# One load moved to another queue, and two groups of VectorE instructions put in another order, in a kernel of linear attention and an MLP

## The chip, the cores and the metric

The kernel runs on one core of a Trainium2 chip. The metric is the device time of one execution in microseconds (us). TensorE (PE in the profile) multiplies matrices, VectorE (DVE), ScalarE (ACT) and GpSimd (POOL) do elementwise work, and SyncE (SP) issues most of the transfers. Each engine runs its own list of instructions in order; engines meet only at semaphores.

## The reference

Inputs are q, k, v of shape (4, 8, 768, 64) in float32 (batch, heads, sequence, head size), one decay `lam` per head, and two weight matrices of 512 x 2048 and 2048 x 512. Attention is linear with decay, in blocks of 64 positions; its output, 3072 tokens of 512 features, goes through an MLP with SiLU:

```python
for b in range(nb):
    intra = np.einsum('bhic,bhjc->bhij', qb, kb) * Dmask[None]
    intra = np.einsum('bhij,bhjd->bhid', intra, vb)
    inter = np.einsum('bhid,bhde->bhie', qb * lam_pow[None], kv_state)
    out[:, :, sl] = intra + inter
    kv_state = lam_block[None, :, None, None] * kv_state + np.einsum('bhsd,bhse->bhde', kb_dec, vb)
...
h = x @ w_in
return (h * (1.0 / (1.0 + np.exp(-h)))) @ w_out
```

## The kernel before

**Tiles.** The 3072 tokens are 24 chunks of 128 (6 per batch entry), and 12 groups of 256 tokens (two chunks) for the MLP. Group g holds chunks 2g and 2g+1. Everything is written out by hand in one order per engine (`tc.manual_schedule()`, line 70): the Python code calls the instructions in the order in which each engine will run them, and nothing is rearranged afterwards.

**Chunks 0 to 3** and groups 0 and 1 go by a list (`ORDER`, line 23). From chunk 4 on the attention of a chunk has these steps:

- *Loads.* `load_qk` (line 884) and `load_v` bring q, k and v of a chunk, 256 KB each, into the buffers `qf`, `kf`, `vf`. By default SyncE issues them; with `e=nc.scalar` ScalarE does, from its own instruction list (line 232). The semaphores of the transfers are used in turn, so that an issue may wait until an earlier transfer with the same semaphore has landed.
- *Preparation.* `prep` (line 377) lets GpSimd scale q and k by powers of the decay into `qb` and `kb`: two instructions each (lines 364 and 365).
- *Transposes.* `dma_t` (line 386) lets SyncE transpose `qb` and `kb` by transfer into `qt` and `kn` (lines 390 and 391). They and the loads stand in one list on SyncE.
- *Values.* `vcast` (line 382) casts v to `vb`, on ScalarE, or on GpSimd for chunks 10 and 11.

**`section`** (line 438) emits the attention's matmuls, all at line 540. For `scores` it computes `sp` from `kn` and `qt` and then multiplies by the mask on VectorE into `ss` (line 560). For `states` it computes key-value products `kv_ps` and lets `sums` (line 565) add them on VectorE to the running state `total` (lines 572 and 574), which is cast to `kvs`. For `outs` it multiplies `ss` by `vb` and `qt` by `kvs` into `op`; that is then copied to `xt`, the input of the MLP. With `defer=True` the sums aren't emitted at once; the caller gets the function and calls it later, and the casts `late` are done later still.

**The MLP of a group** has eight steps `ups` (line 955), each with 16 matmuls (two halves of 8) into a bank `h_ps` (line 613; two banks, tag `h`), and Silu on ScalarE into `g` (line 625). As `g` tiles come, VectorE makes sums and differences of them: `g_diff` (line 715, tile `gd`, line 720) and `g_cross` (line 702, tiles `gc`, line 706, and `gb`, line 708). Steps i = 0, 1, ... 7 take the tiles in the order 0, 1, 4, 5, 2, 3, 6, 7; `g_cross` follows steps 3 and 7, `g_diff` steps 1, 3 and 5. Then `seven` (line 735) does the second product by seven products of half the size, with precomputed sums of weights (`wsum`): products 3 and 4 from `g`, 1 from `gc`, 6 and 7 from `gd`, 5 and 2 from `gb`, all at line 733, 8 matmuls each. VectorE and ScalarE combine them: after product 4, ScalarE copies product 3 to `msum` (line 762), VectorE adds product 4 (line 767) and does the last `g_diff`; after product 6 it adds product 1 (line 771). Product 5 accumulates into the bank of product 3, next to product 4.

**The order around the change.** While groups 0 and 1 finish their second product, chunks 4 to 9 are loaded: chunks 8 and 9 by ScalarE's queue (lines 938 and 947). At line 944 chunks 6 and 7 are prepared and transposed. The loop at line 965 then runs group g's MLP with the attention of the next group between its steps. For g = 2, chunks 8 and 9 are prepared and transposed ahead of step 4 (lines 969, 970), and the section for the scores and states of chunks 6 and 7 stands between products 4 and 1 (line 996), its casts on ScalarE. For g = 3, the section for the scores and states of chunks 8 and 9 stands between steps 5 and 6, with the sums deferred to behind step 6 (lines 977 to 980); their casts on ScalarE come between products 4 and 1. In every group the section that makes the next group's `xt` (and, from g = 3 on, the scores and states of the two chunks after it) stands ahead of product 2 (line 1003).

Of the kernel before, what the change touches and what calls it, by code (L numbers as in the profile page):

```python
# [36 lines left out]
def kernel(  # L37
# [10 lines left out]
    nc = tc.nc  # L48
    B, H, S, D = q.shape
# [126 lines left out]
    def move(e, dst, src):  # L176
        if e == "A":
            nc.scalar.activation(dst, src, AF.Copy)  # L178
        elif e == "P":
            nc.gpsimd.tensor_copy(dst, src)  # L180
        else:
            nc.vector.tensor_copy(dst, src)  # L182
# [44 lines left out]
    rawq, rawk, vraw = {}, {}, {}  # L227

    def load_1(src, c, tag, bufs, e=None):
        b, blk = divmod(c, NB)  # L230
        t = io.tile([128, H, D], F32, name=tag, tag=tag, bufs=bufs)
        (e or nc.sync).dma_start(out=t, in_=src[b, :, blk * BLK:(blk + 1) * BLK, :].rearrange("h s d -> s h d"))
        return t

    def load_k(c, e=None):
        rawk[c] = load_1(k, c, "kf", 6, e)
# [198 lines left out]
    LAG = 220  # L435
    T64 = 32

    def section(outs=(), scores=(), states=(), e="AA", tags=(("att", 3),) * 2, spare=None, cast="D", defer=False):

# [20 lines left out]
        states = [(c, h) for c, h in states if (c + 1) % NB or not h]  # L462
# [9 lines left out]
        def place(c, h):  # L472
            w = [x for x, y in states if y == h].index(c)
            return kv[0][:, h] if shared else kv[h][:, w]
# [72 lines left out]
        if outs:  # L547
            if len(outs) == 2:
                x = xt[group_of[outs[0]][0]]
            for i, op in enumerate(banks):  # L550
                if len(tags) == 4:
                    i, w = divmod(i, 2)
                    move(e[w], x[:, 2 * i:2 * i + 2, BLK * w:BLK * w + BLK], op[:, :, 0, :])
                else:
                    move(e[i], x[:, 2 * i:2 * i + 2, :], op.rearrange("d p w s -> d p (w s)"))
        if scores:
            both = []
            for j, sp in enumerate(sps):
                ss = work.tile([128, len(scores) * NP, D], BF16, name="ss", tag="ss", padded_shape=[128, 2 * NP, D])
                nc.vector.tensor_tensor(ss, sp.rearrange("k w p q -> k (w p) q"),  # L560
                                        mask64[:, None, :].to_broadcast([128, len(scores) * NP, D]), op=AL.mult)
                both.append(ss)
            for w, c in enumerate(scores):
                st[c] = [ss[:, NP * w:NP * w + NP, :] for ss in both]
        def sums():
            casts = []
            for c, h in states:
                b = c // NB
                kvs = nat.tile([128, NP, D], BF16, name="kvs", tag="kvs", bufs=8)
                old, total[b] = total.get(b), nat.tile([128, NP, D], F32, name="total", tag="total", bufs=4)  # L570
                if old is None:
                    nc.vector.tensor_copy(total[b], place(c, h))
                else:
                    nc.vector.tensor_tensor(total[b], old, place(c, h), op=AL.add)  # L574
                casts.append((kvs, total[b]))
                if not defer:
                    move(cast, *casts[-1])
                kvh[(c, 1) if h == 0 else (c + 1, 0)] = kvs
            return casts

        if defer:
            return sums
        sums()

    kvh = {}
    mask64 = const.tile([128, 64], F32, name="mask64")
# [128 lines left out]
    def g_diff(g, j):  # L715

        one = quad(g, j)
        d = sum_tile(g, "gd", j // 2, 128)[:, j % 2]
        a, b = (hi, lo) if j < 2 else (lo, hi)
        nc.vector.tensor_tensor(d, one[:, :, a], one[:, :, b], op=AL.subtract)  # L720
        for u in range(4):
            gs[g, 6 if j < 2 else 7, 4 * (j % 2) + u] = d[:, u, :]
# [12 lines left out]
    def seven(g):  # L735

        last = g == len(GROUPS) - 1
        if last:
            tags = ("o0", 1), ("o1", 1), ("att", 3), ("att", 3), ("h", 2)
# [24 lines left out]
        def after_4():  # L764
            if not last:
                after_3()
            nc.vector.tensor_tensor(m, m, place[4], op=AL.add)
            g_diff(g, 3)

        def after_1():  # L770
            nc.vector.tensor_tensor(m, m, place[1], op=AL.add)
# [31 lines left out]
        if last:  # L803
            order = [(3, True, after_3), (4, True, after_4), (1, True, after_1), (6, True, None),
                     (2, False, last_2), (5, False, last_5), (7, True, last_7)]
        else:
            order = [(3, True, None), (4, False, after_4), (1, True, None), (6, False, after_1),
                     (5, False, None), (2, False, after_2), (7, True, after_7)]

        def step(n, start, after):  # L810
# [73 lines left out]
    def load_qk(*cs, e=None):  # L884
        for c in cs:
            if c < NCHUNK:
                rawq[c] = load_1(q, c, "qf", 4, e)
                load_k(c, e)
                loaded.append(c)
# [31 lines left out]
    def down0(kk, *mts):  # L921
        for mt in mts:
            ffn2(mt // 2, mt % 2, range(4 * kk, 4 * kk + 4), tag="h" if mt > 1 else "o")
# [19 lines left out]
    down0(3, 3)  # L943
    preps(6, 7), transposes(6, 7)
    section((4, 5), (), (), "AD", (("att", 3), ("kv", 1), ("att", 3), ("att", 3)))
    down0(3, 0)
    load_qk(9, e=nc.scalar)
    down0(3, 1)
    for i in range(len(WSUMS)):
        weight_sum(i, 1)  # L950
# [1 line left out]
    def steps(*cs):  # L952
        return [(c, h) for c, h in [(cs[0] - 1, 1)] + [(c, h) for c in cs for h in range(2)] if c > 5][:-1]
# [11 lines left out]
    for g in range(2, len(GROUPS) - 1):  # L965
        c, d, a, b = range(2 * g + 2, 2 * g + 6)
        for i in range(8):
            if g == 2 and i == 4:
                preps(8, 9)
                transposes(8, 9)  # L970
                load_qk(10)
                load_vs(8, 9)
                load_qk(11)
            if g < 4 and i in (4, 5):
                vcast(c + i % 2)
            if g == 3 and i == 6:
                sums = section((), (c, d), steps(c, d), defer=True)
            ups(g, i)
            if g == 3 and i == 6:
                late = sums()  # L980
        for i, unit in enumerate(seven(g)):
            if i == 2 and g > 3:
                vcast(a)
            if i == 2 and g == 3:
                for x in late:
                    move("A", *x)
            if i == 2:
                if g == 3:
                    vcast(a, "P"), vcast(b, "P")
                preps(c + 4, d + 4)  # L990
                transposes(c + 4, d + 4)
                load_qk(*([12] if g == 2 else []), c + 7)
                load_vs(c + 6, d + 6)
                load_qk(d + 7)
            if i == 2 and g == 2:
                section((), (c, d), steps(c, d), cast="A")
            if i == 3 and g > 3:
                vcast(b)
            if i == 0 and g == 2:
                load_vs(10, 11)  # L1000
            if i == 5:
                cs = [x for x in (a, b) if g > 2 and x < NCHUNK]
                section((c, d), cs, steps(*cs) if cs else (), "AD", many[:2] if cs else many, cast="P")
            unit()
    g = len(GROUPS) - 1
# [34 lines left out]
```

## Time and profile before

| | us |
|---|---|
| median of 3 runs | 200.37 |
| lowest and highest | 199.79, 200.69 |
| the profiled execution | 199.81 |
| its span | 198.0 |
| TensorE busy in the span | 188.6 |
| VectorE busy | 133.7 |
| ScalarE busy | 100.9 |
| GpSimd busy | 73.3 |

The profile is of one execution. A row of the timeline has the start, the length, the engine (PEld loads weights; ACTq and SPq are the queues from which ScalarE and SyncE issue transfers), the line and the operation with its output and input, and in brackets the idle time ahead of it with what ended that. Rows of equal instructions that follow each other are merged, with x and their count. Lengths in the timeline include the overlap with the next instruction. The chain of work that ended last has the start, the length and the instruction that the end depended on at that time; there the lengths add up. The waits view has, for a waiting instruction and the one it waited for, the total in us, how often, and the longest. In the DMA view the last number is the time from issue to landing. The granted clock of TensorE was full throughout.

### The profile page before, as it was taken

The numbers are of one execution on the slowest core, as the hardware profiler recorded it, in microseconds if no ns is written. First come the engines' busy times: TensorE is split into PE (matmuls) and PEld (weight loads), VectorE is DVE, ScalarE is ACT, GpSimd is POOL, SyncE is SP. The second block draws the span as 40 slices with busy tenths as digits, with TensorE's granted clock in tenths as the row PEclk, the third lists the DMA queues.
The fourth block names the chain that finished last, engine by engine and source line by source line (L and its number), as shares of the span: only waits on it lengthen the run. The fifth ranks groups of instructions, "written<-read, shape, count | busy, mean of one in ns | idle before, by whom it ended". The sixth has DMA issues, their size and how long they took to land.

```text
span 198.0 us, 6672 instructions
## 1 busy us (share of the span) xinstructions
PE 188.6 (95%) x2844; PEld 151.2 (76%) x2844; DVE 133.7 (68%) x254; ACT 100.9 (51%) x190; POOL 73.3 (37%) x126
## 2 busy tenths in 40 slices
PE   7589999999899998999999999999999999999993
PEld 2368544556787887888888888888888888888882
DVE  0796358679996495984765874895885846745443
ACT  2875875162835653554554563563662662633621
POOL 5240000937942463873614751770850300200000
PEclk9999999999999999999999999999999999999999
DMA  3999999999958998999869999599799850200203
GB/s 92 336 353 403 398 408 333 220 288 281 191 83 198 205 138 198 221 128 211 179 121 244 119 225 173 114 267 162 179 377 243 208 196 7 106 0 3 106 3 106
DMA packets 95581, 38.71 MB, mean 196 GB/s; under 512 B 80960, under 2 KB 88640, under 8 KB 95552
## 3 DMA queue, kind: packets, MB, share of 16 engines
q1 hardware_dynamic: 91248, 37.24, 77.0%
q10 hardware_dynamic: 4304, 1.05, 2.9%
q8 instruction: 22, 0.36, 0.7%
q14 instruction: 7, 0.06, 0.1%
HBM read 27.27 MB, written 6.29 MB: 169 GB/s over the span
## 4 chain that ended last, share of the span: by engine, by line
PE 79%; DVE 11%; SPq 3%; DMA 2%; issue 1%; POOL 1%; ACT 1%; DVEq 0%; POOLq 0%
PE h_ps L613 32%; PE o_ps L733 25%; PE o_ps L658 7%; PE h_ps L847 5%; PE op L540 4%; SPq L224 3%; DVE wsum L689 2%; DMA pair<-in_q_dram 2%; PE o_last L733 2%; DVE gd L720 2%; DVE gb L708 1%; PE sp L540 1%; DVE total L574 1%; DVE ss L560 1%; DVE gc L706 1%
## 5 line engine op out<-in xcount | busy, mean ns | idle before, releaser
L613 PE MATMUL h_ps<-xt,w_in_bf 128*128 128x256 bf16 x672 | 76.1, 272 | 0.8 <-ACT g L625 0.8
L613 PEld LDWEIGHTS <-w_in_bf 128*128 128x128 bf16 x672 | 65.5, 98 | 9.6 <-issue 1.0
L625 ACT ACTIVATE g<-h_ps 128x512 bf16<-128x512 f32 x84 | 49.8, 597 | 34.7 <-PE h_ps L613 34.6
L180 POOL CAST kvs<-total 128x256 bf16<-128x256 f32 x26 | 10.7, 416 | 36.9 <-DVE total L574 27.5
L720 DVE TENSOR_TENSOR gd<-g 128x512 bf16<-128x512 bf16 x40 | 21.7, 557 | 3.4 <-ACT g L625 3.4
L364 POOL TENSOR_TENSOR qb<-qf,lam_fwd 128x256 bf16<-128x256 f32 x18 | 12.8, 709 | 28.5 <-DMA qf<-in_q_dram 21.7
L178 ACT ACTIVATE xt<-op 128x256 bf16<-128x256 f32 (+1 forms) x18 | 8.3, 486 | 22.9 <-PE op L540 22.5
L182 DVE CAST xt<-op 128x256 bf16<-128x256 f32 (+1 forms) x16 | 8.3, 543 | 16.4 <-PE op L540 14.8
L706 DVE TENSOR_TENSOR gc<-g 128x512 bf16<-128x512 bf16 x20 | 10.0, 498 | 13.7 <-ACT g L625 13.6
L733 PE MATMUL o_ps<-w_out_bf,gb 128*128 128x256 bf16 x144 | 18.9, 273 | 0.1
L733 PE MATMUL o_ps<-wsum,gd 128*128 128x256 bf16 x144 | 18.7, 273 | 0.0
L733 PE MATMUL o_ps<-wsum,g 128*128 128x256 bf16 x144 | 17.2, 273 | 0.0
L708 DVE TENSOR_TENSOR gb<-g 128x1024 bf16<-128x1024 bf16 x20 | 17.2, 859 | 0.0
L733 PEld LDWEIGHTS <-gd 128*128 128x128 bf16 x160 | 15.7, 98 | 1.8
L733 PEld LDWEIGHTS <-g 128*128 128x128 bf16 x160 | 15.7, 98 | 1.8
L733 PEld LDWEIGHTS <-gb 128*128 128x128 bf16 x160 | 14.8, 98 | 2.3 <-issue 0.3
L364 POOL TENSOR_TENSOR kb<-kf,lam_bwd 128x256 bf16<-128x256 f32 x20 | 15.0, 748 | 2.2 <-DMA kf<-in_k_dram 1.1
L574 DVE TENSOR_TENSOR total<-total,kv_ps 128x256 f32<-128x256 f32 x33 | 13.8, 419 | 2.2
L658 PE MATMUL o_ps<-w_out_bf,g 128*128 128x512 bf16 x64 | 14.8, 379 | 0.0
L365 POOL TENSOR_TENSOR kb<-kf,lam_bwd 128x256 bf16<-128x256 f32 x20 | 14.8, 740 | 0.0
L365 POOL TENSOR_TENSOR qb<-qf,lam_fwd 128x256 bf16<-128x256 f32 x18 | 13.0, 724 | 0.0
L560 DVE TENSOR_TENSOR ss<-sp,mask 128x512 bf16<-128x512 f32 x20 | 12.8, 681 | 0.2 <-PE sp L540 0.2
(106 smaller groups left out, 245.8 us busy)
## 6 DMA issues: line engine op xcount, KB each, us to landing
vf<-in_v_dram SPq DMA_DIRECT2D x20, 256.0 KB, 4.6
kf<-in_k_dram SPq DMA_DIRECT2D x18, 256.0 KB, 5.2
pair<-in_moe_w_out_dram SPq DMA_DIRECT2D x8, 512.0 KB, 7.7
qf<-in_q_dram SPq DMA_DIRECT2D x16, 256.0 KB, 4.3
pair<-in_moe_w_in_dram SPq DMA_DIRECT2D x6, 512.0 KB, 7.1
out_dram<-pair SPq DMA_DIRECT2D x12, 256.0 KB, 3.4
out_dram<-ob SPq DMA_DIRECT2D x10, 256.0 KB, 2.9
pair<-in_k_dram SPq DMA_DIRECT2D x4, 256.0 KB, 4.5
```

The source lines that it names most:

```text
L180: nc.gpsimd.tensor_copy(dst, src)
L364: eng.tensor_tensor(dst[:, 0::2], src[:, 0::2, ::-1, :], by[:, 0::2, ::-1, :], op=AL.mult)
L365: eng.tensor_tensor(dst[:, 1::2], src[:, 1::2], by[:, 1::2], op=AL.mult)
L560: nc.vector.tensor_tensor(ss, sp.rearrange("k w p q -> k (w p) q"), mask64[:, None, :].to_broadcast([128, len(scores) * NP, D]), op=AL.mult)
L574: nc.vector.tensor_tensor(total[b], old, place(c, h), op=AL.add)
L613: nc.tensor.matmul(hps[g, i][:, a:a + 256], lhsT=w_in_bf[:, ko, m * 128:(m + 1) * 128], rhs=xt[g][:, ko, :], start=(ko == 0 and u == 0), s ...
L625: nc.scalar.activation(gg.rearrange("p u n -> p (u n)"), hps[g, i], AF.Silu)
L658: nc.tensor.matmul(o, lhsT=gt[g, ko][:, mt * BLK:(mt + 1) * BLK], rhs=w_out_bf[:, ko, :], start=(ko == 0), stop=(ko == KO_OUT - 1))
L706: nc.vector.tensor_tensor(cross, low[:, :, lo], one[:, :, hi], op=AL.add)
L708: nc.vector.tensor_tensor(both, low, one, op=AL.add)
L720: nc.vector.tensor_tensor(d, one[:, :, a], one[:, :, b], op=AL.subtract)
L733: nc.tensor.matmul(dst, lhsT=lhsT, rhs=rhs, start=(start and k == 0), stop=(k == K2 - 1), skip_group_check=True)
```

## The change

Three edits, none of which adds or removes arithmetic.

1. The k load of chunk 9 is issued by SyncE and not by ScalarE. Its place in SyncE's list is behind the transposes of chunks 6 and 7 and ahead of those of chunks 8 and 9. The q load of chunk 9 stays with ScalarE, in the same place of its list.
2. In the section for chunks 6 and 7 (g = 2) VectorE does the three state sums ahead of the two masks, and the last `g_diff` of the group, which stood ahead of both, now follows both.
3. In g = 3 the deferred state sums of chunks 8 and 9 (four) are emitted behind step 7 and not behind step 6, so that `gc` and `gb` of step 7 come ahead of them on VectorE.

The instruction lists of TensorE and GpSimd have the same instructions in the same order as before; ScalarE's has one transfer less, SyncE's one more.

```diff
-    def section(outs=(), scores=(), states=(), e="AA", tags=(("att", 3),) * 2, spare=None, cast="D", defer=False):
+    def section(outs=(), scores=(), states=(), e="AA", tags=(("att", 3),) * 2, spare=None, cast="D", defer=False, early=False):
...
-        if scores:
+        def masked():
             both = []
...
+        if early:
+            sums()
+        if scores:
+            masked()
         if defer:
             return sums
-        sums()
+        if not early:
+            sums()
...
             nc.vector.tensor_tensor(m, m, place[4], op=AL.add)
-            g_diff(g, 3)
+            if g != 2:
+                g_diff(g, 3)
...
-            order = [(3, True, None), (4, False, after_4), (1, True, None), (6, False, after_1),
+            order = [(3, True, None), (4, False, after_4), (1, True, (lambda: g_diff(g, 3)) if g == 2 else None), (6, False, after_1),
                      (5, False, None), (2, False, after_2), (7, True, after_7)]
...
     section((4, 5), (), (), "AD", (("att", 3), ("kv", 1), ("att", 3), ("att", 3)))
+    rawq[9] = load_1(q, 9, "qf", 4, nc.scalar)
     down0(3, 0)
-    load_qk(9, e=nc.scalar)
+    load_k(9)
     down0(3, 1)
...
             ups(g, i)
-            if g == 3 and i == 6:
+            if g == 3 and i == 7:
                 late = sums()
...
             if i == 2 and g == 2:
-                section((), (c, d), steps(c, d), cast="A")
+                section((), (c, d), steps(c, d), cast="A", early=True)
```

## The prediction, made blind

> **What bounds the kernel now.** I read the page first: its span and the chain that ended last. The profiled execution took 199.81 us, of which the span is 198.0 and 1.8 lies around it.
>
> ```profile
> span 198.0 us, 6672 instructions
> ...
> PE 79%; DVE 11%; SPq 3%; DMA 2%; issue 1%; POOL 1%; ACT 1%; DVEq 0%; POOLq 0%
> ```
>
> TensorE holds 79% of the chain, VectorE 11%. An edit that touches no matmul can only win time where TensorE waits, or where VectorE is the chain. So the second view is TensorE's waits; asked for 41 to 77 us, it has these three rows.
>
> ```profile
> PE h_ps L613 <- ACT g L625: 0.8, 1, 0.8
> PE o_ps L733 <- DVE gc L706: 0.6, 1, 0.6
> PE op L540 <- ACT kvs L178: 0.2, 1, 0.2
> ```
>
> Each of the three edits aims at one of these rows; I price them in order of time from the timeline and the chain. I call the three places A (49 us), B (61 us) and C (74 us). From 77 us to the end the same view, asked for that window, names no TensorE wait, so what is won at A to C stays, if the loads keep up.
>
> **The change part by part.**
>
> *Place A: k of chunk 9 leaves ScalarE's queue.* Timeline, and the landing of one load from the DMA view:
>
> ```profile
> 42.76 0.54 ACTq L232 DMA_DIRECT2D kf<-in_k_dram  x1
> ...
> 47.41 1.91 PE L613 MATMUL h_ps<-xt,w_in_bf 128*128 128x256 bf16 x16
> ...
> 49.05 0.37 ACTq L232 DMA_DIRECT2D kf<-in_k_dram  x1
> 49.47 1.08 ACT L625 ACTIVATE g<-h_ps 128x512 bf16<-128x512 f32 x2 [3.14 <-PE h_ps L613]
> ...
> 50.12 5.64 PE L613 MATMUL h_ps<-xt,w_in_bf 128*128 128x256 bf16 x48 [0.79 <-ACT g L625]
> ```
>
> ```profile
> kf<-in_k_dram ACTq DMA_DIRECT2D x1, 256.0 KB, 6.2
> ```
>
> The k load of chunk 9 shares a semaphore with the k load of chunk 8, and waits for it: that one was issued at 42.76 and took 6.2, so it landed at 48.96; the next issue follows at 49.05. Silu stands behind it in ScalarE's order and starts at 49.47. TensorE's first h tile (8 of the 16 matmuls of the 47.41 row, half of 1.91) was ready about 48.4, so the profile's releaser for the 3.14 is misleading. Without the load, Silu runs from about 48.4 and lasts half of 1.08; its bank is free at 49.0, before TensorE's second tile ends at 49.3. The 0.79 us goes, at no cost on ScalarE. It costs SyncE one issue, priced below. What is late next is VectorE, which runs without a pause from 48 to 61 us; hence place B.
>
> *Place B: state sums of 6 and 7 ahead of the masks, g_diff behind both.* The chain, with the unstalled section of chunks 4, 5 first, then timeline rows:
>
> ```profile
> 44.94 0.80 PE op L540 x64
> ...
> 55.60 1.51 DVE gd L720 x2
> ...
> 57.45 0.60 DVE gb L708
> 58.05 0.33 DVE msum L767
> 58.38 0.34 DVE gd L720
> 58.72 1.20 DVE ss L560 x2
> 59.92 0.34 DVE total L572
> ...
> 61.19 0.42 ACT kvs L178
> ```
>
> ```profile
> 57.54 0.38 ACT L762 ACTIVATE msum<-o_ps 128x256 f32<-128x256 f32 x1 [1.15 <-PE o_ps L733]
> ...
> 60.78 0.25 PE L540 MATMUL op<-ss,vb 64*64 64x64 bf16 x8
> ...
> 62.20 1.05 PE L733 MATMUL o_ps<-w_out_bf,gb 128*128 128x256 bf16 x8
> ```
>
> The section's 64 matmuls take 0.80 when nothing is late; here 1.42 pass between 60.78 and 62.20, so 0.62 is stall, for the last of three casts kvs behind the three totals. With A gone TensorE is at the section at 60.78 - 0.79 = 59.99. VectorE's new order is msum, three totals (59.92 to 61.17: 1.25), masks (1.20), gd (0.34).
>
> If VectorE came no earlier than before, msum would end at 58.38, the totals at 59.63, the masks at 60.83: TensorE waits there, the section ends 0.8 later at 61.63 and not 62.20, and A and B together win 0.57. That is the low bound. But kb of chunk 9 must now wait for a later load (below), so GpSimd pauses from 55 to about 57 us. The two gd at 55.60 cost 0.76 each beside GpSimd's work and 0.34 alone at 58.38: 0.84 less; a little of the gb ahead too, about 0.2. VectorE is then through gb at about 57.0. ScalarE's msum copy (57.54 - 0.79 + 0.33 = 57.08) comes just behind, so msum ends at 57.4, the totals at 58.7, the masks at 59.9, and the last kvs at 59.1. All precede 59.99. I take the full 0.62; it has 0.1 us to spare. The moved gd is ready at 60.3 and is read at about 61.7 (a product of 8 matmuls behind the one at 62.20 - 1.41), so the move itself is free; were it late, it would cost what it is late.
>
> *Place C: gc and gb ahead of the state sums of 8 and 9.*
>
> ```profile
> 68.99 1.02 DVE gb L708
> ...
> 72.72 0.34 DVE total L574
> ...
> 74.41 0.35 DVE gc L706
> ```
>
> ```profile
> 71.19 1.36 POOL L180 CAST vb<-vf 128x512 bf16<-128x512 f32 x2
> ...
> 72.04 0.60 ACT L625 ACTIVATE g<-h_ps 128x512 bf16<-128x512 f32 x1 [0.22 <-PE h_ps L613]
> ...
> 74.80 0.61 PE L733 MATMUL o_ps<-wsum,gc 128*128 128x256 bf16 x4 [0.62 <-DVE gc L706]
> ...
> 76.12 1.04 PE L733 MATMUL o_ps<-w_out_bf,gb 128*128 128x256 bf16 x8
> ```
>
> Four totals (72.72 to 74.41: 1.69) stand ahead of gc, and TensorE waits 0.62 for it. In the new order that wait goes: gc can start when Silu of the last tile ends (72.04 + 0.55). But the first matmul with gb, at 76.12, waits for VectorE's msum (it accumulates into a bank that msum reads; the built program has this wait), and msum still stands behind the totals. VectorE now idles until that Silu instead of doing totals. On the new clock (1.41 earlier): Silu ends at 71.2; gc 0.35, gb 0.60, totals 1.69, msum 0.33 end at 74.2 when GpSimd is quiet. GpSimd isn't: its two casts of vb (71.19 to 72.55) don't move earlier, and lie on gc and gb; gd and gb cost 0.42 more each when beside GpSimd (0.76 against 0.34, 1.02 against 0.60), so the other end is 75.0. TensorE wants 76.12 - 0.62 - 1.41 = 74.09. The new wait is 0.1 to 0.9; I take 0.5, the middle. C wins 0.62 - 0.5 = 0.1, with bounds 0.5 and -0.3.
>
> *The Trainium skill on this place:* SBUF — State Buffer, section Who interferes with whom, says that a VectorE instruction with two SBUF inputs contends with a GpSimd instruction that reads SBUF, and that the later one is fully blocked until the other ends. The 0.76 against 0.34 agrees that there is contention; no row says how much a cast blocks. By that rule gc and gb could each lose a whole cast; that is the second rival.
>
> *What the moved load does to SyncE.* SyncE issues in order and without a pause here; timeline, then landings:
>
> ```profile
> 52.30 1.22 SPq L391 DMA_TRANSPOSE kn<-kb  x1
> ...
> 58.41 1.20 SPq L391 DMA_TRANSPOSE kn<-kb  x1
> 59.65 0.58 SPq L232 DMA_DIRECT2D qf<-in_q_dram  x1
> ...
> 72.94 1.21 SPq L391 DMA_TRANSPOSE kn<-kb  x1
> ```
>
> ```profile
> 56.03 0.79 POOL L365 TENSOR_TENSOR kb<-kf,lam_bwd 128x256 bf16<-128x256 f32 x1
> ...
> 77.49 0.22 PE L540 MATMUL sp<-qt,kn 64*64 64x64 bf16 x2
> ```
>
> ```profile
> qf<-in_q_dram SPq DMA_DIRECT2D x1, 256.0 KB, 3.2
> kn<-kb SPq DMA_TRANSPOSE x1, 2.4
> ```
>
> The load goes out at 53.6, behind the transposes of 6 and 7. The nearest row is the q load at 59.65, also right behind four transposes: 3.2 to land, so 56.8. The far row is the 6.2 above: 59.8. GpSimd then makes kb of 9 in about 1.2 (the 56.03 row ended at 56.82 before, and would end at 58.0), SyncE transposes it (the 58.41 row), and all later loads and transposes queue behind. Their delay d is 0.6 (one issue of 0.58) if SyncE is the limit, a little below zero if the wait inside the earlier transposes absorbs it; it grows to landing minus 57.2 when the load is late (59.8 gives 2.6). The first consumer that can feel d is the scores of chunks 10, 11: the last transpose for them was issued at 72.94 and landed at 75.34; TensorE's matmuls on it begin about 77.49. So there are 2.1 us of slack, which the win uses up: **no more than 2.1 - d can be won**, 1.5 with d = 0.6.
>
> **Sum:** 0.79 + 0.62 + 0.1 = 1.5, and the load's limit is 1.5 as well. Against the profiled 199.81 that is 198.3. The median of the runs shown, 200.37, lies 0.56 above that execution, so the median should fall to 198.9.
>
> **Rivals.**
>
> 1. *The late load becomes the bound, slower than before.* Place: GpSimd's kb of 9, then SyncE's transpose of it, then the scores of 10, 11. It decides the sign where d passes 2.1, that is where the load lands after 59.3, 5.7 us behind its issue. With the 6.2 of the row above d is 2.6 and the time 0.5 longer: 200.3, or 200.9 as a median. For it: that very row. Against: it was taken among the loads of chunks 6 to 8, the 3.2 in the emptier stretch where the load now goes. 7%. A milder case, landing at 58 to 59, leaves 0.3 to 1.3: about 199.0, median 199.6. 13%.
> 2. *A new wait at C eats A's win.* If gc and gb each wait for a whole cast (1.36 for the two, in place of the 0.4 of my middle case), msum ends about 75.6, TensorE waits 1.5, C loses 0.9, and 0.5 is left: 199.3, median 199.8. For it: the casts stay where they are while VectorE comes earlier. Against: only one cast may overlap. 12%.
> 3. *The change doesn't do what it says*: VectorE, not the load or the order, still ends the stretch to 61 us, because GpSimd's pause doesn't help it. A and B give 0.57, C 0.1: 199.1, median 199.7. 10%.
> 4. *All three waits vanish* (0.79 + 0.62 + 0.62 = 2.0; d near zero, casts off gc and gb): 197.8, median 198.4. 10%.
>
> **How the numbers follow.** My forecast, a win of 1.1 to 1.9, holds 48%. A measurement of this kernel can tell 0.5%, about 1.0 us, from no change. Faster by more: the forecast, rival 4 and half of the milder case of rival 1, 65%. Within: rivals 2 and 3 and the other half, 28%. Slower: 7%. The predicted time is 198.9. The range goes from 198.0 (rival 4, with the scatter of the runs, which reach 0.6 below their median) to 200.2 (the mild cases of rivals 1 to 3); outside it stay the slower case and a few in a hundred on either side.
>
> **What would show it.** Right: no ScalarE DMA issue at 49 us and Silu near 48.4; no TensorE wait at 50.1; the section of 6 and 7 in 0.8 to 0.9; the wait for gc gone, and a TensorE wait of up to 0.9 for msum ahead of the first matmul with gb of the next group; kb of 9 on GpSimd near 57. Wrong: kb of 9 later than 58.5, or TensorE waiting for a transpose at the scores of 10, 11 or 12, 13: then the load costs more than I took. A wait ahead of the section of 6 and 7 for the masks would say that VectorE did not gain from GpSimd's pause. If the waits went as forecast and the time did not, a load further on must have come late.

## The result, and the profile after

| | before | after |
|---|---|---|
| median, us (13 runs each) | 199.54 | 198.70 |
| lowest | 198.76 | 197.94 |
| profiled execution | 199.81 | 198.77 |
| its span | 198.0 | 196.9 |

The ratio is 0.9941 with an interval of 0.9916 to 0.9966: faster by 1.2 us (0.7 to 1.7). Ratios here leave out, on both sides, the executions more than 1.5% above the fastest of their kernel, so they need not be the quotient of two medians: these two medians differ by 0.8, and in the repeat below (a2_again), where four of 12 are out against two of 35, the medians hardly differ. The prediction was 198.9, with a range of 198.0 to 200.2. The 0.59% lies just over the 0.5% that a measurement can tell from no change; the interval reaches below that mark.

In the changed kernel the lines have other numbers: h_ps 619 (before 613), Silu 631 (625), the second product 739 (733), `gc` 712 (706), `gb` 714 (708), `gd` 726 (720), `msum` 773 (767), the totals 573 and 575 (572 and 574). One figure of the section on the kernel needs mending: a step of the MLP has 8 matmuls in two halves of 4, not 16 (a group's eight steps are the x64 below); the prediction's working uses 8.

The page of the changed kernel, its chain by engine:

```profile
span 196.9 us, 6669 instructions
...
PE 85%; DVE 5%; SPq 2%; DMA 2%; issue 2%; POOL 1%; ACT 1%; DVEq 0%; POOLq 0%
```

VectorE's share of the chain fell from 11% to 5%, TensorE's rose from 79% to 85%. TensorE's waits of the changed kernel from 44 to 82 us (waiting instruction, what it waited for, us in total, times, longest):

```profile
PE o_ps L739 <- DVE msum L773: 0.3, 1, 0.3
PE o_ps L664 <- issue: 0.2, 1, 0.2
```

The three waits of before are gone (for `g`, `gc` and `kvs`), and the new one for `msum` that the prediction named is there. Next, the timeline of the changed kernel through places A and B:

```profile
47.97 7.39 PE L619 MATMUL h_ps<-xt,w_in_bf 128*128 128x256 bf16 x64
49.05 0.60 ACT L631 ACTIVATE g<-h_ps 128x512 bf16<-128x512 f32 x1 [2.16 <-PE h_ps L619]
...
52.73 0.53 SPq L232 DMA_DIRECT2D kf<-in_k_dram  x1
...
54.30 0.41 DVE L712 TENSOR_TENSOR gc<-g 128x512 bf16<-128x512 bf16 x1
54.63 0.68 DVE L714 TENSOR_TENSOR gb<-g 128x1024 bf16<-128x1024 bf16 x1
55.24 0.75 DVE L726 TENSOR_TENSOR gd<-g 128x512 bf16<-128x512 bf16 x2
55.75 0.71 POOL L364 TENSOR_TENSOR kb<-kf,lam_bwd 128x256 bf16<-128x256 f32 x1 [1.65 <-DMA kf<-in_k_dram]
56.02 0.72 DVE L712 TENSOR_TENSOR gc<-g 128x512 bf16<-128x512 bf16 x1
56.42 0.79 POOL L365 TENSOR_TENSOR kb<-kf,lam_bwd 128x256 bf16<-128x256 f32 x1
56.66 1.10 DVE L714 TENSOR_TENSOR gb<-g 128x1024 bf16<-128x1024 bf16 x1
...
59.26 1.28 DVE L560 TENSOR_TENSOR ss<-sp,mask 128x512 bf16<-128x512 f32 x2
...
60.59 0.25 PE L540 MATMUL op<-ss,vb 64*64 64x64 bf16 x8
61.37 1.05 PE L739 MATMUL o_ps<-w_out_bf,gb 128*128 128x256 bf16 x8
```

Place A is one row: 64 matmuls without a gap (how much of this is owed to the change is told with b2 and b3). Silu follows the first tile at 49.05, 1.08 behind its start. Between GpSimd's instructions VectorE runs fast (54.30 to 55.99); from 55.75 on k of chunk 9 is on GpSimd, and `gc` and `gb` of the last step take 0.72 and 1.10 instead of 0.41 and 0.68. That makes the masks end at 60.54, and the section's matmuls on `ss` start at 60.59. Place C of the same timeline:

```profile
71.83 0.42 DVE L712 TENSOR_TENSOR gc<-g 128x512 bf16<-128x512 bf16 x1 [0.49 <-ACT g L631]
72.17 0.68 DVE L714 TENSOR_TENSOR gb<-g 128x1024 bf16<-128x1024 bf16 x1
72.56 0.76 POOL L180 CAST vb<-vf 128x512 bf16<-128x512 f32 x1 [0.82 <-DMA vf<-in_v_dram]
72.77 1.78 DVE L575 TENSOR_TENSOR total<-total,kv_ps 128x256 f32<-128x256 f32 x4
73.33 1.21 SPq L391 DMA_TRANSPOSE kn<-kb  x1
74.46 0.41 DVE L773 TENSOR_TENSOR msum<-msum,o_ps 128x256 f32<-128x256 f32 x1
74.93 1.03 PE L739 MATMUL o_ps<-w_out_bf,gb 128*128 128x256 bf16 x8 [0.28 <-DVE msum L773]
```

VectorE idles until Silu, does `gc` and `gb` undisturbed, then the four totals and `msum`; TensorE waits 0.28 for that.

**A table by stage.** For all traces I cut the time by the starts of TensorE's rows. *Start* is the first h matmul of group 2 (47.41 before, 47.97 after). A runs from there to product 3 of group 2 (55.60 and 55.20); B from its product 5 to its product 2 (59.82 to 62.20, 59.42 to 61.37); C from product 1 of group 3 to its product 5 (73.58 to 76.12, 72.74 to 74.93); D from there to its product 2; *rest* from there to the end of the span. The stretches between A and B (4.22) and between B and C (11.37 or 11.38) are the same (within 0.01) in all traces but three: e10_split and e8_early (5.05 and 5.83 between A and B) and e6_late (13.19 between B and C). The runs are those of the experiments.

| trace | start | A | B | C | D | rest |
|---|---|---|---|---|---|---|
| before | 47.41 | 8.19 | 2.38 | 2.54 | 2.20 | 119.68 |
| after | 47.97 | 7.23 | 1.95 | 2.19 | 2.19 | 119.78 |
| a2_again | 49.60 | 7.23 | 1.83 | 2.19 | 2.19 | 119.96 |
| b2 | 48.98 | 7.22 | 2.96 | 2.26 | 2.20 | 119.68 |
| b3 | 47.72 | 9.38 | 2.39 | 2.49 | 2.19 | 119.83 |
| b_delay | 48.75 | 7.96 | 2.39 | 1.83 | 2.19 | 119.38 |
| e1_load | 47.43 | 7.22 | 2.54 | 2.14 | 2.20 | 120.48 |
| e2_section | 47.52 | 8.13 | 2.29 | 2.60 | 2.19 | 120.07 |
| e3_sums | 48.99 | 7.23 | 2.39 | 2.19 | 2.19 | 119.51 |
| e12_no_sums | 49.90 | 7.22 | 1.84 | 2.27 | 2.19 | 119.48 |
| e9_msum | 47.96 | 7.22 | 1.84 | 1.74 | 2.80 | 119.94 |
| e8_early | 47.42 | 7.23 | 1.74 | 2.40 | 2.83 | 121.38 |
| e6_late | 47.45 | 7.23 | 1.98 | 2.60 | 2.19 | 119.64 |
| e10_split | 47.80 | 7.23 | 1.74 | 1.74 | 2.97 | 119.99 |

In the pair before and after, A won 0.96, B 0.43 and C 0.35: 1.74 between 47 and 78 us. Of that, 0.56 was lost ahead of 47 us, where no instruction was changed, and 0.10 behind 78 us; 1.1 is left, as the spans say. These are differences of two single executions; means over the traces stand further down, under the sum. The start is scatter of single executions: group 0's h matmuls begin between 17.21 and 18.78 in the traces of before and of kernels with its code ahead of them, between 17.21 and 18.02 in those of the changed family. A theory that the change itself made the start later fell by these rows.

### The profile page after: what moved, and what is told of

Same layout as the page of the kernel before. It is cut to its first block, busy times and chain, and to the rows that moved or that the text cites. A ratio compares the mean times of both kernels' runs of the same rounds, so it can differ in the third digit from the quotient of the medians.

```text
span 196.9 us, 6669 instructions
## 1 busy us (share of the span) xinstructions
PE 187.8 (95%) x2840; PEld 150.7 (77%) x2844; DVE 131.9 (67%) x254; ACT 101.4 (51%) x190; POOL 72.2 (37%) x126
## 4 chain that ended last, share of the span: by engine, by line
PE 85%; DVE 5%; SPq 2%; DMA 2%; issue 2%; POOL 1%; ACT 1%; DVEq 0%; POOLq 0%
PE h_ps L619 38%; PE o_ps L739 25%; PE o_ps L664 7%; PE h_ps L854 5%; PE op L540 4%; SPq L224 2%; DMA pair<-in_q_dram 2%; PE o_last L739 2%; PE sp L540 2%; DVE total L575 1%; PE kv_ps L540 1%; DVE gb L714 1%; ACT g L631 1%; DVE ss L560 1%; POOL vp L253 1%
## 5 line engine op out<-in xcount | busy, mean ns | idle before, releaser
L364 POOL TENSOR_TENSOR qb<-qf,lam_fwd 128x256 bf16<-128x256 f32 x18 | 11.8, 657 | 32.4 <-DMA qf<-in_q_dram 22.2
L726 DVE TENSOR_TENSOR gd<-g 128x512 bf16<-128x512 bf16 x40 | 19.5, 500 | 4.0 <-ACT g L631 4.0
L712 DVE TENSOR_TENSOR gc<-g 128x512 bf16<-128x512 bf16 x20 | 10.5, 525 | 15.2 <-ACT g L631 15.0
L364 POOL TENSOR_TENSOR kb<-kf,lam_bwd 128x256 bf16<-128x256 f32 x20 | 14.2, 709 | 4.5 <-DMA kf<-in_k_dram 4.4
L365 POOL TENSOR_TENSOR kb<-kf,lam_bwd 128x256 bf16<-128x256 f32 x20 | 14.9, 744 | 0.0
L664 PE MATMUL o_ps<-w_out_bf,g 128*128 128x512 bf16 x60 | 14.1, 379 | 0.4 <-issue 0.3
L365 POOL TENSOR_TENSOR qb<-qf,lam_fwd 128x256 bf16<-128x256 f32 x18 | 12.4, 690 | 0.0
```

The costliest lines, as they stand in the source:

```text
L364: eng.tensor_tensor(dst[:, 0::2], src[:, 0::2, ::-1, :], by[:, 0::2, ::-1, :], op=AL.mult)
L365: eng.tensor_tensor(dst[:, 1::2], src[:, 1::2], by[:, 1::2], op=AL.mult)
L664: nc.tensor.matmul(o, lhsT=gt[g, ko][:, mt * BLK:(mt + 1) * BLK], rhs=w_out_bf[:, ko, :], start=(ko == 0), stop=(ko == KO_OUT - 1))
```

## The experiments

The theory was the prediction's: three separate stalls go, for the reasons given there, and the moved load has room. The rivals were that the section or the sums alone do it, that the new order only moves a wait, and that the load is near a limit. Kernels that were timed have 12 runs unless a number is given; before has 35, 35 or 23 runs beside them.

### The parts alone

**e1_load**: before with edit 1 alone.

```diff
+    rawq[9] = load_1(q, 9, "qf", 4, nc.scalar)
     down0(3, 0)
-    load_qk(9, e=nc.scalar)
+    load_k(9)
```

> Edit 1 alone: k of chunk 9 from SyncE, VectorE's orders as before. Theory (three separate TensorE stalls, VectorE just behind the first): A goes whole, so the stretch from the first matmul of group 2's first MLP product to its first with wsum is 7.2 us and not 8.2. At B the old order gives part of it back: masks, totals and casts end at about the same time as before, the section of chunks 6 and 7 takes 1.2 to 1.6 and not 0.8, B loses up to 0.2. C: the wait for gc is 0.2 to 0.6. Sum 0.8 to 1.2 us faster than before. Rival (the stalls are one chain on VectorE, and the load by itself wins nothing): within 0.3 us of before. Rival (the load alone is the whole gain): 1.7 us in the stretch from 47 to 78 us, as in the changed kernel.

Median 199.55 against 200.01, ratio 0.9993 [0.9956, 1.003]: not told from no change. A lost its stall (7.22), but B gave 0.16 back, and TensorE's waits of this kernel, first from 44 to 82 us, then from 78 to the end, show what took its place:

```profile
PE op L540 <- ACT kvs L178: 0.4, 2, 0.2
PE o_ps L733 <- DVE gc L706: 0.2, 1, 0.2
...
PE sp L540 <- DMA kn<-kb: 0.6, 1, 0.6
```

The wait of 0.6 for a transpose is at the scores of chunks 12, 13 (91.55 us): the loads came later behind the moved one, and took part of the gain back. In this trace A, B and C together are 1.21 shorter than before, about as expected (0.8 to 1.2), and 0.80 of that is lost again behind 78 us.

**e2_section**: the changed kernel without edits 1 and 3, so before with edit 2 alone.

```diff
-    rawq[9] = load_1(q, 9, "qf", 4, nc.scalar)
     down0(3, 0)
-    load_k(9)
+    load_qk(9, e=nc.scalar)
...
-            if g == 3 and i == 7:
+            if g == 3 and i == 6:
                 late = sums()
```

> Edit 2 alone: state sums of 6 and 7 ahead of the masks, last g_diff behind both; load and deferred sums as before. Theory: A's stall of 0.79 stays; TensorE reaches the section as late as before, VectorE's masks end at about the same moment (58.4 + 1.25 + 1.2 = 60.8), so the section takes 0.8 and its wait for kvs goes: 0.5 to 0.6 faster. C unchanged. Sum 0.5 us faster. Rival (the casts kvs are not what holds the section): no difference.

Median 199.33, ratio 0.9974 [0.9945, 1.0003]. Its timeline:

```profile
57.13 0.83 DVE L712 TENSOR_TENSOR gc<-g 128x512 bf16<-128x512 bf16 x1
...
60.06 1.28 DVE L560 TENSOR_TENSOR ss<-sp,mask 128x512 bf16<-128x512 f32 x2
...
61.39 0.26 PE L540 MATMUL op<-ss,vb 64*64 64x64 bf16 x8 [0.48 <-DVE ss L560]
```

B won only 0.09, where 0.5 to 0.6 was expected. The wait for `kvs` turned into one of 0.48 for the masks, since GpSimd made k of chunk 9 beside VectorE until 57.7 (the last `gc` 0.83; in the trace of before GpSimd was through at 56.8, and this `gc` took 0.41). So in this execution the new order lacked the pause that edit 1 makes on GpSimd. How late GpSimd is without edit 1 scatters by such amounts, and this is one trace. A keeps its stall (8.13).

**e3_sums**: before with edit 3 alone.

```diff
-            if g == 3 and i == 6:
+            if g == 3 and i == 7:
                 late = sums()
```

> Edit 3 alone: gc and gb ahead of the four state sums of 8 and 9; load and section as before. Theory: the wait of 0.62 for gc goes, and a new wait of 0.2 to 0.3 for msum (behind the totals) comes ahead of the first matmul with gb; 0.3 to 0.4 us faster. Rival (whole casts of GpSimd block gc and gb): the new wait is 1 or more and the kernel is slower by 0.4 or more. Rival (no new wait): 0.6 faster.

Median 199.77, ratio 0.9997 [0.9967, 1.0027]. C won 0.35, with the new wait as expected, but A's stall was absent from this execution, which no theory had foreseen. Its timeline:

```profile
48.99 0.37 ACTq L232 DMA_DIRECT2D kf<-in_k_dram  x1
...
50.06 0.60 ACT L625 ACTIVATE g<-h_ps 128x512 bf16<-128x512 f32 x1 [2.16 <-PE h_ps L613]
...
76.40 1.03 PE L733 MATMUL o_ps<-w_out_bf,gb 128*128 128x256 bf16 x8 [0.29 <-DVE msum L767]
```

TensorE started group 2 at 48.99 here and not at 47.41, so ScalarE was through the issue at 49.36, before its first tile was ready. That asked for the tests of A below.

**e12_no_sums**: the changed kernel without edit 3 (the second hunk of e2_section alone).

> Edits 1 and 2 without 3. Theory: A and B as in the changed kernel (1.4 us from 47 to 62 us). At C, with TensorE 1.4 us earlier and VectorE's masks of 8 and 9 ended before the last Silu, the totals fill VectorE's pause; gc is then at most 0.1 to 0.5 late, and there is no wait for msum: C is worth 0.1 to 0.5, so the time is that of the changed kernel within 0.3 us. That would say that edit 3 brings nothing once 1 and 2 are made. Rival (edit 3 is worth its whole 0.35 us): slower than the changed kernel by 0.35 or more, with the wait of 0.6 for gc back.

Median 198.66, ratio 0.9953 [0.9926, 0.9979]. In its timeline TensorE waits for `gc` again, but only 0.34:

```profile
75.50 0.61 PE L739 MATMUL o_ps<-wsum,gc 128*128 128x256 bf16 x4 [0.34 <-DVE gc L712]
```

C is 2.27 against 2.19: with edits 1 and 2 in, edit 3 is worth 0.08. The two intervals overlap almost whole. Without edit 3 C scatters from 2.14 to 2.60 (before, b2, b3, e1_load, e2_section and this run, mean 2.38); with it C is 2.19 in all three traces in which the sums and the load are not moved further (the changed kernel's two, e3_sums). So the 0.35 of the pair is a draw, and 0.2 the mean.

**a2_again**: the changed kernel once more, for the scatter.

> The changed kernel once more, for a second trace and for the comparison with the three kernels beside it. Theory: the 0.56 us that its first trace lost ahead of 47 us (where no instruction was changed) is scatter between executions; in this trace the start of group 2's MLP lies anywhere between 47.2 and 48.2, and from there to the end the time is 1.7 us shorter than before. Rival (the change costs time at the start, by the layout of the code): the start is again at 48.0.

Median 200.29 against 200.33, ratio 0.9948 [0.9904, 0.9992]. As a repeat of the gain this is weak, since the two medians hardly differ; what repeats is the trace. A, B and C are as in the first trace (7.23, 1.83, 2.19). Its start, 49.60, lay outside what was expected; the page's line of the granted clock and the timeline say why:

```profile
PEclk9997899999999999999999999999999999999999
```

```profile
17.87 5.19 PE L619 MATMUL h_ps<-xt,w_in_bf 128*128 128x256 bf16 x32
```

The clock fell to 0.7 to 0.8 from 15 to 25 us, and 32 matmuls that take 3.67 in the trace of before took 5.19. e12_no_sums has the same (5.33), and the latest start, 49.90.

### Does the stall at A belong to the order, or is it a race?

**b2** and **b3** are the kernel before, one execution each, for a trace.

> The kernel before once more, for a second trace. Theory (A's stall depends on when TensorE arrives): if group 2's MLP starts at 47.4 to 47.6, the stretch to the first matmul with wsum is 8.1 to 8.2; if it starts at 48.9 or later, 7.2; between, the difference. Rival: 8.2 whatever the start.

> The same a third time, with the same expectations: 8.1 to 8.2 for a start at 47.4 to 47.6, 7.2 for one at 48.9 or later.

They took 200.68 and 201.37. Timeline of b2, then of b3:

```profile
49.20 0.42 ACTq L232 DMA_DIRECT2D kf<-in_k_dram  x1
...
50.05 0.60 ACT L625 ACTIVATE g<-h_ps 128x512 bf16<-128x512 f32 x1 [2.16 <-PE h_ps L613]
```

```profile
50.54 0.39 ACTq L232 DMA_DIRECT2D kf<-in_k_dram  x1
50.98 1.09 ACT L625 ACTIVATE g<-h_ps 128x512 bf16<-128x512 f32 x2 [4.35 <-DMA kf<-in_k_dram]
```

b2 started at 48.98 and has no stall (A 7.22), as expected. b3 started at 47.72; a stall of 0.9 to 1.0 was expected and A is 9.38, a stall of 2.16, since the load of chunk 8 landed later. So both sides of the race scatter: TensorE's start, and the landing that frees ScalarE's issue (7.2 behind the load's issue in b3, 6.2 before, 5.4 in b2). The stall is the start of Silu less 1.08 and less the start of group 2: 49.47 - 48.49 = 0.98 before, 50.98 - 48.80 = 2.18 in b3, 0 in b2. With the load in ScalarE's list and no other work added, five traces (before, b2, b3, e2_section, e3_sums) have an A of 8.03 in the mean, 0.81 above 7.22. With the load on SyncE all eight traces have 7.22 or 7.23.

But most of these eight would have had no stall in any case. In the changed kernel's first trace, timeline and DMA view:

```profile
42.31 0.54 ACTq L232 DMA_DIRECT2D kf<-in_k_dram  x1
```

```profile
kf<-in_k_dram ACTq DMA_DIRECT2D x1, 256.0 KB, 5.5
```

Chunk 8's k landed at 47.8. Before, Silu started 0.51 behind that landing (48.96 and 49.47); here that would be 48.3, ahead of the first tile at 49.05. So with the load in its old place this execution would have had no stall at A either (an estimate), and the 0.96 of the pair is what the trace of before happened to draw. The same estimate for the other traces in which the DMA view tells this landing: no stall in a2_again (48.2), e1_load (48.0) and e9_msum (47.7), 1.2 in e8_early (49.2), 0.7 in e6_late (48.7). With before, b2, b3, e2_section and e3_sums that makes eleven draws, six of them without a stall; their mean, 0.55, is the estimated worth of edit 1 at A.

**b_delay**: before, with TensorE held up by 1.3 us ahead of place A: six more matmuls of `zero`, which add nothing to their bank.

```diff
+        if (g, mt) == (0, 0) and kos[0] == 0:
+            for _ in range(6):
+                nc.tensor.matmul(o, lhsT=zero[:, :BLK], rhs=zero, start=False, stop=False, skip_group_check=True)
```

> The kernel before with six more matmuls (zeros added to an accumulation, 512 columns each, about 1.3 us) ahead of the first matmuls of group 0's second product, at 31 us; the output stays the same. Theory (A's stall is a race between TensorE and the landing of chunk 8's k load, so it shrinks when TensorE comes late): TensorE reaches group 2's MLP about 1.3 us later, the wait of 0.8 for Silu is gone, the stretch to the first matmul with wsum is 7.2 and not 8.2, and the kernel is only 0.3 to 0.6 us slower than before. Rival (the stall belongs to the order of the instructions alone): 8.2 again, 1.3 us slower.

Median 201.14 (10 runs) against 200.76, ratio 1.0025 [0.9992, 1.0058]: 0.5 slower (-0.2 to 1.2) for 1.3 us of added work, as expected. But the stall did not vanish. Its timeline, and the landing of chunk 8's k from the DMA view:

```profile
42.42 0.54 ACTq L232 DMA_DIRECT2D kf<-in_k_dram  x1
...
50.16 0.38 ACTq L232 DMA_DIRECT2D kf<-in_k_dram  x1
50.59 1.08 ACT L625 ACTIVATE g<-h_ps 128x512 bf16<-128x512 f32 x2 [2.93 <-DMA vf<-in_v_dram]
```

```profile
kf<-in_k_dram ACTq DMA_DIRECT2D x1, 256.0 KB, 5.6
```

Chunk 8's k landed at 48.0, and a Silu 0.51 behind that would not have been late. The issue of chunk 9's k went out at 50.16 only, because in this build it stands behind the semaphore of another transfer, the v load that the last row names; in all the traces of before it is that of chunk 8's k. So the added matmuls also changed which landing ScalarE waits for, and the run is not the test it was meant to be. It shows once more that Silu follows the issue (50.59, 0.43 behind it): A still had 0.74 of stall at a start of 48.75. C shrank to 1.83 instead: a TensorE that is late waits less for VectorE.

### What comes behind the wait for msum

**e9_msum**: the changed kernel with the sums moved further back, behind product 1.

```diff
-            if g == 3 and i == 7:
-                late = sums()
...
             if i == 2 and g == 3:
+                late = sums()
                 for x in late:
```

> The changed kernel with the four state sums of 8 and 9 moved once more, behind msum and the last g_diff of group 3. Theory (the new wait at C is msum behind the totals): the wait of 0.28 ahead of the first matmul with gb goes; the totals end 0.4 later, their casts kvs by about 75.5, in time for the section near 75.7: 0.2 to 0.3 us faster than the changed kernel. Rival: the wait moves to the casts kvs or to the section's kv_ps bank, no difference.

Median 199.12 against 200.33, ratio 0.9934 [0.9906, 0.9962]. C lost its wait (1.74), D rose from 2.19 to 2.80, because the casts `kvs` now come behind the totals:

```profile
76.20 0.22 PE L540 MATMUL op<-qt,kvs 64*64 64x64 bf16 x2 [0.23 <-ACT kvs L178]
```

C and D together are 4.54 against 4.38 in the changed kernel: in this trace the wait moved and nothing was won, as the rival had it. The timing does not contradict that (0.9934 against 0.9948, with intervals that overlap), and does not prove it.

**e10_split**: the changed kernel with two of the four sums behind step 6 and two behind product 1.

```diff
-        def sums():
+        def sums(lo=0, hi=None):
...
-            for c, h in states:
+            for c, h in states[lo:hi]:
...
-            if g == 3 and i == 7:
-                late = sums()
+            if g == 3 and i == 6:
+                late = sums(0, 2)
...
             if i == 2 and g == 3:
+                late += sums(2)
                 for x in late:
```

> The changed kernel with the four deferred state sums split: two stand behind step 6 of group 3, in the pause that VectorE has ahead of the last Silu, and two behind msum and the last g_diff. Theory (at C three things must be on time: gc at 73.2, msum at 74.5, the casts kvs near 75.5): with two totals on either side all three are; the stretch from product 1 to the product behind the section is 3.9 to 4.0 us, against 4.74 before and 4.38 in the changed kernel: 0.4 faster than the changed kernel, 1.5 to 2 faster than before. Rival (VectorE has not the time for all of it): one of the three waits stays at 0.2 or more, and no gain over the changed kernel.

Median 199.79 against 200.76, ratio 0.9965 [0.9939, 0.9991]. B and C are both 1.74, the least of all traces: VectorE holds TensorE up nowhere in them. For B that is no merit of the split, which changes nothing ahead of it: TensorE came to B 0.8 later than its start would have it, because in this trace it waited for transposes:

```profile
57.83 0.32 PE L540 MATMUL sp<-qt,kn 64*64 64x64 bf16 x16 [0.64 <-DMA kn<-kb]
...
77.11 0.22 PE L540 MATMUL sp<-qt,kn 64*64 64x64 bf16 x2 [0.62 <-DMA kn<-kb]
```

The first is for chunks 6, 7 and makes the stretch between A and B 5.05 long and not 4.22; the second, for chunks 10, 11, makes D 2.97. The first wait is not in the other traces with the same code up to there (after, a2_again, e9_msum, e12_no_sums), so it is a draw of SyncE's transfers; where VectorE is on time, SyncE's list can be next. This version isn't told from the changed kernel by its timing, and shows no gain over it.

### Where in SyncE's list the load may stand

**e8_early**: the changed kernel with the load ahead of the transposes of 6 and 7.

```diff
+    load_k(9)
     preps(6, 7), transposes(6, 7)
...
     down0(3, 0)
-    load_k(9)
```

> The changed kernel with k of chunk 9 earlier in SyncE's list, ahead of the transposes of 6 and 7. Theory (B is won because GpSimd pauses for this load while VectorE does gd, gc, gb): GpSimd makes kb of 9 without the pause, at 54 to 56 us; gc, gb, gd of group 2 cost 0.7 to 1.0 each again, the masks of 6 and 7 end 0.4 to 0.8 later, the section waits for them; 0.4 to 0.8 slower than the changed kernel up to 62 us. Rival (the pause is of no account; the load is better early): same or faster by up to 0.3.

Median 200.42 against 200.33, ratio 0.9997 [0.9959, 1.0035]: no gain is left to be seen. Its trace is long also from 79 us on, where no edit stands (the rest, 121.38), so only its order and its waits up to there are read:

```profile
46.28 2.87 SPq L232 DMA_DIRECT2D kf<-in_k_dram  x1
49.25 2.11 SPq L390 DMA_TRANSPOSE qt<-qb  x1
...
55.11 1.59 DVE L726 TENSOR_TENSOR gd<-g 128x512 bf16<-128x512 bf16 x2
...
58.22 0.32 PE L540 MATMUL sp<-qt,kn 64*64 64x64 bf16 x16 [1.42 <-DMA kn<-kb]
```

VectorE's rows grew as the theory said (`gd` 1.59 for two, against 0.75: GpSimd no longer pauses). But the larger loss is another, which neither theory had named: the issue occupied SyncE for 2.87, the transposes began at 49.25 and not at 45.98, and TensorE waited 1.42 for them. The profile puts the length of that issue down to ScalarE's first Silu of group 2, which ended at 49.10; why the load should wait for it stays open. Because TensorE came late, its B is 1.74 and the masks held nothing up: the run is no test of the pause.

**e6_late**: the changed kernel with the load behind the transposes of chunk 8.

```diff
-    load_k(9)
...
-                preps(8, 9)
-                transposes(8, 9)
+                preps(8)
+                transposes(8)
+                load_k(9)
+                preps(9)
+                transposes(9)
```

> The changed kernel with k of chunk 9 later in SyncE's list, behind the transposes of 8: it goes out 2.6 us later, lands at about 58.5, and SyncE's loads of 10 and 11 come 1.5 to 2 us later. Theory (2.1 - d): B gains up to 0.2, since gc and gb of group 2 are free of GpSimd; but the last transpose for the scores of 10, 11 lands at about 77.3 where TensorE wants it near 76.2, a new wait of 0.8 to 1.4; 0.6 to 1.2 us slower than the changed kernel, about as before. Rival (the loads have slack to spare): as fast as the changed kernel or 0.2 faster.

Median 202.12 against 200.33, ratio 1.0068 [1.003, 1.0105]: slower than before. Its timeline:

```profile
56.60 0.54 SPq L232 DMA_DIRECT2D kf<-in_k_dram  x1
...
59.87 0.61 POOL L364 TENSOR_TENSOR kb<-kf,lam_bwd 128x256 bf16<-128x256 f32 x1 [5.09 <-DMA kf<-in_k_dram]
...
62.68 0.58 SPq L232 DMA_DIRECT2D qf<-in_q_dram  x1
...
68.81 0.32 PE L540 MATMUL kv_ps<-vb,kb 64*64 64x64 bf16 x16 [0.40 <-ACT vb L178]
70.31 0.32 PE L540 MATMUL kv_ps<-vb,kb 64*64 64x64 bf16 x16 [1.19 <-ACT vb L178]
76.67 1.03 PE L739 MATMUL o_ps<-w_out_bf,gb 128*128 128x256 bf16 x8 [0.70 <-DVE msum L773]
```

The load goes out 3.9 later than in the changed kernel, and every load behind it follows late (q of chunk 10 at 62.68 against 59.34). That such a delay turns the win into a loss is what the prediction's limit said, but the first consumer that felt it was another: not the scores of 10, 11, but the values of 8 and 9, whose loads stand in SyncE's list behind the moved one. TensorE waited 0.40 and 1.19 for `vb`, and the stretch from B to C is 13.19 long. The 0.70 ahead of the first matmul with `gb` is C's new wait where a cast of GpSimd does fall on `gb` (which took 1.10 here, and 0.68 in the changed kernel).

## Why the prediction was right, and where it was not

**Place A: the mechanism is right, its size is a draw.** 0.79 was taken; the profiled pair gave 0.96. The reason given (the issue behind the landing of chunk 8's load holds Silu) is shown by before, b2, b3, e2_section and e3_sums, where Silu starts with the first tile or 0.42 to 0.44 behind the issue, whichever is later. What the prediction did not see is that one trace is one draw from 0 to 2.2; the estimated mean is 0.55. Each stall also costs 0.17 or 0.18 more in its stretch than its bracket says: 8.19 - 7.22 - 0.79 here, 2.54 - 1.74 - 0.62 at C before, 2.19 - 1.74 - 0.28 at C after.

**Place B: 0.43 in place of 0.62.** The step that missed is "it has 0.1 us to spare". To compare clocks, take 0.56 off the rows of the changed kernel, by which its group 2 starts later. VectorE was then on time: the totals ended at 58.7 (59.26 - 0.56) and the masks at 59.9 (60.45 - 0.56), as forecast. TensorE was early: it would have been at the section at 59.82 and not at 59.99 (product 5 at 59.42, and 0.96 from there to the section as before, less 0.56), since A's stall had cost 0.17 more than its bracket. So the masks came last, and 0.2 of stall remained (1.95 against 1.74). A and B together gave 1.39 where 1.41 was forecast: what A won above its price, B lost.

That VectorE met the forecast is in part luck, because two misses cancel. The load went out at 52.73 and not at 53.6, since SyncE's first transpose held it for less (2.52 against 3.44); so GpSimd's `kb` came at 55.75 and not at 56.8, on top of the last `gc` and `gb`, which lost 0.31 and 0.42. But GpSimd's pause also began earlier, at 54.10 and not at 55, and the first `gc` and `gb` won 0.84 by it (0.41 and 0.68, against 0.83 and 1.10 before), where 0.2 was taken. The working had only asked what a later load costs, not what an earlier one falls on.

**Place C: 0.35 in place of 0.1.** The new wait was named and placed rightly, and its 0.28 lies in the 0.1 to 0.9 of the text; the 0.5 taken from the middle was too much for this execution. No cast of v fell on `gc` or slowed `gb`: the first had ended at 71.74, just ahead of `gc`, and the second waited 0.82 for its own load (72.56). Where one does, as in e6_late, the wait is 0.70. Rival 2 gave each of the two a whole cast: `gc` took 0.42 and `gb` 0.68, so nothing of it came about. By the rule of the Trainium skill, SBUF — State Buffer, Who interferes with whom, the later of the two is fully blocked until the other ends. The rows at 55.75 to 57.76 agree with that but for 0.13 each: `gc` began with 0.44 of GpSimd's first instruction left (until 56.46) and took 0.31 longer than alone, `gb` with 0.55 of the second left (until 57.21) and took 0.42 longer. So what is lost is what is left of the other instruction, which need not be a whole one.

**The load's limit: right in kind, wrong in place.** d was taken as 0.6. The last transpose for chunks 10, 11 was issued at 73.33 against 72.94, d = 0.4, while this execution's TensorE had started 0.56 later; no transpose was waited for. In e1_load, whose group 2 starts as early as before, d is 1.0 (73.96), and a wait of 0.6 for a transpose came at the scores of 12, 13. e10_split met the limit at the scores of 10, 11 (0.62), e6_late at the values of 8, 9, which the working had passed over.

**The sum.** 0.96 + 0.43 + 0.35 is 1.7 against 1.5 in the stretch that the change touches; A's and B's errors are one and cancel, and C's is left. The median fell by 1.2 in ratio, 0.3 less than forecast; the forecast lies inside its interval. That the median, 198.70, lies so near the 198.9 is in part luck: the forecast took its 1.5 off the median of 3 runs, 200.37, which over 13 runs is 199.54. Means over the traces give another check, as an estimate: A 0.55; B 0.67, from 2.53 (before, b2, b3, e1_load, e3_sums) to 1.87 (both traces of the changed kernel, e12_no_sums, e9_msum); C 0.2; together 1.4. Rival 1's sign was right for a load 3.9 later (e6_late). Rival 3 fell: `gd` took 0.75 for two beside a quiet GpSimd. Rival 4 did not come about, and e10_split, which has neither wait on VectorE, is no faster.

**Open.** The forecast's 1.5 and the traces' 1.4 both lie inside the timing's 0.7 to 1.7, which can't tell them apart. Executions also lose time elsewhere: e1_load 0.8 behind 78 us, the changed kernel 0.1 and 0.3 in two traces. The places are coupled: b2 has no stall at A, and its B is 2.96, 0.58 more than before, because TensorE is at the section 0.97 sooner after the start of group 2 and VectorE's totals only 0.39. The parts do not add up by their own medians, all three of which are within scatter of before (0.9993, 0.9974, 0.9997). That edit 2 needs edit 1 rests on single traces (B 2.29 with edit 2 alone, 1.84 in e12_no_sums with both) and is likely, not shown.

## What to carry to other kernels

A transfer whose issue must wait should not stand in the list of an engine that computes: here it held Silu by 0 to 2.2 us, by chance of the landing and of TensorE's start. One profile shows only one draw of such a stall, so take a few traces before pricing it, and in the traces after the change ask whether the stall would have been there without it. When a load is moved in a queue, go through every consumer of every transfer behind it, in order of time, and ask what an earlier landing collides with as well as what a later one delays. When one wait goes, write down who is next (here `gc`, then `msum`, then `kvs`, then the transposes): two rounds of that moved VectorE's waits or took them away, and showed no further gain.

## What the runs showed of the hardware

- The same 256 KB load of chunk 8 landed 5.4 behind its issue in b2, 6.2 before and 7.2 in b3; k of chunk 9, issued ten us later, landed in 2.9 in the changed kernel and in 4.4 in e1_load.
- Two builds of almost the same kernel can put the same issue behind different transfers: with six matmuls more (b_delay) the k load of chunk 9 waited for a v load and not for chunk 8's k.
- The granted clock fell to 0.7 to 0.8 from 15 to 25 us in a2_again, and 32 matmuls took 5.19 and not 3.67; the same rows took 5.33 in e12_no_sums.
- VectorE and GpSimd slow each other: `gc` took 0.41 alone and up to 0.83 beside GpSimd, `gb` 0.68 and 1.10, so up to 0.42 more each, whatever their own length; GpSimd's half of `kb` took 0.61 alone, 0.79 beside those and 1.06 beside the longer `wsum` (51.45, before). The masks, which read the matmuls' results, took 1.28 for two beside GpSimd's casts (71.44, before) and with GpSimd idle (59.26, after).
